# Contiguous pieces in SBUF for a fused attention and two-layer kernel: w_in, v, q/k, x and the gated tile laid out anew

## The chip, the cores and the metric

The kernel runs on one core of a Trainium2 chip. The metric is device time in microseconds. TensorE is called PE below (PEld is its weight load), VectorE DVE, ScalarE ACT, GpSimd POOL and SyncE SP. SBUF is the on-chip memory that holds the tiles, PSUM the banks into which PE writes.

## The reference

Attention over 4 batches, 8 heads, 768 positions and 64 channels a head, where each query sees the first 4 positions (the sinks) and its own last 128; then two layers with a squared ReLU between them, over all 3072 tokens.

```python
scores = (1.0 / np.sqrt(D)) * np.matmul(q, k.transpose(0, 1, 3, 2))
keep = (pos[None, :] < 4) | ((rel >= 0) & (rel < 128))       # rel = query - key
a = softmax(np.where(keep, scores, -1e9))
x = np.matmul(a, v).transpose(0, 2, 1, 3).reshape(B * S, H * D)     # 3072 x 512
h = x @ w_in                                                 # 512 x 2048
out = (np.maximum(h, 0.0) ** 2) @ w_out                      # 2048 x 512
```

## The kernel before

**Tiles.** A batch is 768 tokens: six tiles of 128 (index t), three pairs of tiles (index s), four pairs of heads (index m). For batches 0 and 1, SP loads q and k as FP32 (tile qr), they are cast and regrouped to bf16 (qs, on DVE, ACT or POOL), PE transposes them (pt), and ACT and DVE copy the result to qkT. For batches 2 and 3, the tuple NATURAL, POOL's queue loads them with a cast (qn), and SP issues DMA transposes from qn to qkT (the "turns", L416). The values come as FP32 (vf) and are cast to v, or in batches 2 and 3 straight to v by POOL's queue.

**Steps.** For each pair s and each half of the heads: scores on PE (ps, L538), exponential on ACT (expm, L557), mask by a product on DVE (L566) or by a select on POOL (L221), values on PE (po, L599), and a division by the sum on DVE (rc and xn_sb, L610 and L611). Scores of the sinks are a product of their own (pk, L498), whose left operand kblk is copied from qkT by DVE (L481), followed by the sinks' values vs (L484). The x of a pair is turned by PE (px, L634) and copied to xT, or by a DMA transpose in batches 2 and 3. The first layer is pm (L657), ReLU on ACT (r, L666), the square on DVE into gT_sb (L673). The second layer is py (L697), copied out to osb and stored by SP.

**Buffers.** The attention of a batch shares two PSUM slots (`att`) among pt, ps, po, px and pk; pm and py share two others (`den`). So the next scores wait until ACT has read the last.

**What sets the order.** The whole program is recorded as operations with costs, and `Plan.run` places them greedily by start time and key. On each engine the instructions then run strictly in that order. The attention of batch b+1 is spread between the two layers of batch b. The costs in the operations are figures of the planner; they decide the order alone. Waits are put in by the framework, for each pair of instructions whose regions of a tile it takes to overlap.

**Queues.** POOL's queue first loads w_in in four blocks of 512 columns, then w_out in four; block 0 of w_in waits for a q load, and w_out 2 waits for the q and k of batch 0's second group. The loads of batch 2 on POOL's queue stand behind the load of v for batch 1, tile 3. SP's queue carries the q, k and v of batches 0 and 1, then the stores and the turns. Semaphores DMASW0 to 7 count landings of POOL's queue in rotation (so DMASW0 to 3 are first the four blocks of w_in), DMAHW0 to 7 those of SP's.

Of the kernel before, what the change touches and what calls it, by code (L numbers as in the profile page):

```python
# [132 lines left out]
def kernel(  # L133
# [23 lines left out]
    NSINK = 4  # L157
# [18 lines left out]
    head_rows = consts.tile([32, H, 1], BF16)  # L176
    w_in_sb = consts.tile([128, NKB, DFF], BF16)
    w_out_sb = consts.tile([128, NFB, DM], BF16)
# [3 lines left out]
    vs_in = consts.tile([32, B, D + 1], FP32)  # L182
    qkT_all = [consts.tile([128, NP, 2, S], BF16, name=f"qkT{i}") for i in range(2)]
    v_sb = [consts.tile([128, H, NT, D + 1], BF16, name=f"v{i}") for i in range(2)]
    xn_sb = consts.tile([128, NT, DM], BF16)
    xT_sb = [consts.tile([128, NKB, S], BF16, name=f"xT{i}") for i in range(2)]
    gT_sb = consts.tile([128, NFB, S], BF16)

# [90 lines left out]
    def dma_op(queue, name, run, us, behind=None, takes=(), yields=()):  # L279

        def go(e):
            ds = run(e)
            if behind is not None:
                for d in ds:
                    after_dma(d, loaded[behind])
            loaded[name] = ds[-1]
        o = op(-5, {queue: (0.85 if queue == "pool" else 0.5) + (1.5 if behind else 0.0)}, go, dma=us, takes=takes,
               follow=[chained[queue]] if queue in chained else (),
               after=[ops[behind]] if behind is not None else ())
        ops[name] = chained[queue] = o  # L290
        o.yields += [ops[y] for y in yields]
        o.follow += [ops[y] for y in yields]
        return o

    def load_w_in(i, behind=None, yields=()):
        c = slice(512 * i, 512 * i + 512)
        w_in_op[i] = dma_op(
            "pool", ("w_in", i),
            lambda e: [nc.gpsimd.dma_start(out=w_in_sb[:, :, c],  # L299
                                           in_=moe_w_in[:, c].rearrange("(a p) f -> p a f", p=128))],  # L300
            3.1, behind, yields=yields)

    def load_w_out(i, behind=None, yields=()):
        w_out_op[i] = dma_op(
            "pool", ("w_out", i),
            lambda e: [nc.gpsimd.dma_start(
                out=w_out_sb[:, 4 * i:4 * i + 4, :],
                in_=moe_w_out[512 * i:512 * i + 512, :].rearrange("(p f) m -> p f m", p=128))],
            2.8, behind, yields=yields)

# [7 lines left out]
    GROUPS[0] = [(0, 4), (512, 2)]  # L318
    ROW = {256: 0.0205, 512: 0.028, 1024: 0.046, 1536: 0.065}

# [32 lines left out]
    def load_natural(b, s, older_values):  # L353

        begun = [ops["layer1", b - 2, 0, 0], w_out_op[3]]
        for ti in (1, 0):
            if s == 0:
                qn_slot[b, ti] = Slot("qr", NT)
            for i in range(2):
                t = 2 * s + i  # L360

                def run(e, t=t, ti=ti):
                    if t == 0:
                        qn_t[b, ti] = work["qr"].tile([128, NT, DM], BF16, name="qn", tag="qr")
                    return [nc.gpsimd.dma_start(  # L365
                        out=qn_t[b, ti][:, t, :].rearrange("p (h d) -> p h d", d=D),
                        in_=(q, k)[ti][b, :, 128 * t:128 * t + 128, :].rearrange("h p d -> p h d"))]
                o = dma_op("pool", ("qk", b, ti, t), run, 64 * 0.032,
                           ("v", 1, 3) if (b, ti, t) == (2, 1, 0) else None,
                           [qn_slot[b, ti]] if t == 0 else ())  # L370
                o.after += begun
        for t in (2 * s, 2 * s + 1):
            def run(e, t=t):
                return [nc.gpsimd.dma_start(  # L374
                    out=v_sb[b % 2][:, :, t, 0:D],
                    in_=v[b, :, 128 * t:128 * t + 128, :].rearrange("h p d -> p h d"))]
            o = dma_op("pool", ("v", b, t), run, 64 * 0.032)
            o.after += begun + older_values
# [6 lines left out]
    def attention(b, key):  # L385
# [9 lines left out]
        older_layer1 = [ops[x] for x in ops if x[0] == "layer1" and x[1] == b - 2]  # L395
        qkT_sb = qkT_all[b % 2]
        es, vs, vb, kb, xT = es_sb[b % 2], vs_sb[b % 2], v_sb[b % 2], kblk[b % 2], xT_sb[b % 2]

        def stage(g, f0, f1, side):
# [9 lines left out]
            if b in NATURAL:  # L409
                for s in range(NS):  # L410
                    for ti in (1, 0):
                        for i in range(2):
                            t = 2 * s + i

                            def turn(e, s=s, ti=ti, i=i, t=t):
                                nc.sync.dma_start_transpose(  # L416
                                    out=qkT_sb[:, :, ti, 128 * t:128 * t + 128], in_=qn_t[b, ti][:, t, :])
                            ops["turn", b, ti, t] = op(
                                at(0.1 * s), {"sp": 1.25}, turn, dma=0.3, reads=[qn_slot[b, ti]],
                                after=[ops["qk", b, ti, t]] + prev_scores + prev_sinks)  # L420
                            copies.append(ops["turn", b, ti, t])
                    ops["cast", b, s] = ops["v", b, 2 * s + 1]
            for m in range(NP) if b not in NATURAL else ():
# [31 lines left out]
                for ti in (1, 0):  # L455
                    def unload(e, m=m, ti=ti):

                        pt = bank_t[b, m, g]
                        copy(e,
                             qkT_sb[:, m, ti, t0:last].rearrange("c (p t) -> c p t", t=n),  # L460
                             pt[:, ti, 0:128 * n].rearrange("c (t p) -> c p t", t=n))
# [6 lines left out]
            for s in range(t0 // 256, last // 256) if b not in NATURAL else ():  # L468
                def cast(e, s=s):
                    copy(e, vb[:, :, 2 * s:2 * s + 2, 0:D].rearrange("p h t d -> p t h d"), vf_t.pop((b, s)))  # L470
                ops["cast", b, s] = op(at(0.3 + 0.5 * (256 * s - t0) / (last - t0)),
# [5 lines left out]
            if g == 0:  # L477
                def sink_operands(e):
                    for h2 in range(2):
                        r = slice(64 * h2, 64 * h2 + 64)  # L480
                        nc.vector.tensor_copy(  # L481
                            out=kb[r, :].rearrange("p (m c) -> p m c", c=136)[:, :, 4 * h2:4 * h2 + NSINK],
                            in_=qkT_sb[r, :, 1, 0:NSINK])
                    nc.vector.tensor_tensor(  # L484
# [9 lines left out]
            def sink_scores(e):  # L494
                ps = bank_t["sink", b] = bank(bk, "pk", [128, 512], FP32)
                warm(ps[:, 0:128])
                for m in range(NP):
                    nc.tensor.matmul(ps[:, 0:last - lo], lhsT=kb[:, 128 * m:128 * m + 128],  # L498
                                     rhs=qkT_sb[:, m, 0, lo:last],
                                     start=(m == 0), stop=(m == NP - 1))  # L500
# [12 lines left out]
            for s in range(t0 // 256, last // 256):  # L513
                fs = 0.36 + 0.5 * (256 * s - t0) / (last - t0)
                norms = []
                for m0 in (0, 2):
# [4 lines left out]
                    def scores(e, ms, s=s, m0=m0, banks=banks):  # L521
                        for m in ms:
# [12 lines left out]
                            for i, (o, c, qb, w) in enumerate(segs):  # L535
                                for h2 in range(2):
                                    r = slice(64 * h2, 64 * h2 + 64)
                                    nc.tensor.matmul(  # L538
                                        ps[:, h2, o:o + w],
                                        lhsT=qkT_sb[r, m, 1, 128 * c:128 * c + 128],  # L540
                                        rhs=qkT_sb[r, m, 0, 128 * qb:128 * qb + w],
                                        start=(i == 0 and not biased), stop=(i == len(segs) - 1))
# [39 lines left out]
                    def values(e, s=s, m0=m0, bo=bo):  # L582
                        po = bank_t["o", b, s, m0] = bank(bo, "po", [128, 2, 512], FP32)
                        warm(po[:, 0, 0:128])
                        for j, m in enumerate((m0, m0 + 1)):
# [3 lines left out]
                            for h2 in range(2):  # L589
                                h = 2 * m + h2  # L590
                                for i in range(2):
                                    t = 2 * s + i
                                    if t >= 1:
                                        mms.append((i, h2, x[:, h2, 256 * i:256 * i + 128], vb[:, h, t - 1, :]))
                                    mms.append((i, h2, x[:, h2, 256 * i + 128:256 * i + 256], vb[:, h, t, :]))
                                    if t >= 2:
# [22 lines left out]
                if b in NATURAL:  # L619
                    for t in (2 * s, 2 * s + 1):  # L620
                        def turn_x(e, t=t):
                            nc.sync.dma_start_transpose(out=xT[:, :, 128 * t:128 * t + 128], in_=xn_sb[:, t, :])
                        o_ = op(at(fs + 0.36), {"sp": 1.25}, turn_x, dma=0.3, after=norms + older_layer1 +
# [16 lines left out]
                def bridge_copy(e, s=s):  # L640
                    copy(e, xT[:, :, 256 * s:256 * s + 256], bank_t["x", b])
                ops["xT", b, s] = op(at(fs + 0.37), {"dve": 1.2, "act": 1.05}, bridge_copy,
# [4 lines left out]
    def layer1(b, key, fbs, c0, cw, need):  # L647
# [5 lines left out]
        def mm(e):  # L653
            pm = bank_t[tag] = bank(bs, "pm", [128, n, cw], FP32)
            for i, fb in enumerate(fbs):
                for kb in range(NKB):
                    nc.tensor.matmul(pm[:, i, :], lhsT=w_in_sb[:, kb, 512 * (fb // 4) + fb % 4:512 * (fb // 4) + 512:4],  # L657
                                     rhs=xT[:, kb, c0:c0 + cw], start=(kb == 0), stop=(kb == NKB - 1))
        a = op(key, {"pe": n * NKB * cw / 2380.0}, mm, takes=[bs],
# [11 lines left out]
        def square(e):  # L671
            r = bank_t.pop((tag, "r"))
            (nc.vector if e == "dve" else nc.gpsimd).tensor_mul(  # L673
                gT_sb[:, fbs[0]:fbs[0] + n, c0:c0 + cw], r, r)
        ops["sq", b, fbs[0], c0, cw] = op(key, {"dve": 0.7}, square, reads=[rs],
                                      after=[ra] + [ops[x] for x in ops if x[0] == "layer2" and x[1] == b - 1])

    def layer2(b, u, keys, by_part=False):
# [8 lines left out]
        for n, (i, part) in enumerate(order):  # L687
            t = 2 * u + i

            def mm(e, i=i, t=t, part=part, n=n):  # L690
# [5 lines left out]
                for fb in range(4 * part, 4 * part + 4):  # L696
                    nc.tensor.matmul(pm[:, i, :], lhsT=gT_sb[:, fb, 128 * t:128 * t + 128],  # L697
                                     rhs=w_out_sb[:, fb, :], start=(fb == 0), stop=(fb == NFB - 1))
# [127 lines left out]
```

## Time and profile before

| | |
|---|---|
| time, median of 3 runs | 242.93 us (240.55 to 243.56) |
| the profiled execution's own time | 241.31 us |
| its span | 239.6 us |
| PE busy | 224.4 us, 94% |
| ACT, DVE, POOL busy | 115.1, 106.9, 53.8 us |
| first layer pm, 576 matmuls | 89.8 us busy |
| second layer py, 384 matmuls | 89.0 us busy |

PE is the busy engine, but its share is a mean: the page's slices show it idle in two places, and there another engine or a transfer ends last. Busy time also holds matmuls that ran at half clock. The span is the time from the first to the last instruction; 1.7 us of the execution's time lie outside it.

### The profile page before, as it was taken

How to read it: one execution, taken by the hardware profiler on the slowest of the kernel's cores; microseconds unless marked ns; L12 is line 12 of the kernel's file. 1: busy time of each engine (PE TensorE's matmuls, PEld its weight loads, DVE VectorE, ACT ScalarE, POOL GpSimd, SP SyncE). 2: the span in 40 equal slices, each digit the busy share in tenths (PEclk: the TensorE clock that was granted, in tenths of full speed). 3: DMA queues.
4: the chain of work that ended last, by engine and by line, in shares of the span. 5: the costliest groups of instructions: out<-in, count | busy, mean ns of one | idle time of the engine just before them, and what ended most of it. 6: DMA issues, size and time to landing. Idle time of an engine off the chain costs nothing.

```text
span 239.6 us, 4590 instructions
## 1 busy us (share of the span) xinstructions
PE 224.4 (94%) x1944; PEld 142.8 (60%) x1944; DVE 106.9 (45%) x199; ACT 115.1 (48%) x130; POOL 53.8 (22%) x74
## 2 busy tenths in 40 slices
PE   7994699999999769999999999999999999999993
PEld 7654599545994355555458754559645644694441
DVE  5676033335687763656335633857402422431010
ACT  2583056640764764955348445686604226560020
POOL 5250050520693497175000004100000000000000
PEclk9999599999999997999999999999999999999999
DMA  5999899998599999999977513120002512000042
GB/s 186 281 207 209 181 254 175 335 307 159 179 145 108 134 166 150 126 148 151 139 81 206 105 22 80 54 44 4 0 0 73 171 22 90 0 0 3 0 176 88
DMA packets 82021, 29.70 MB, mean 124 GB/s; under 512 B 70224, under 2 KB 78416, under 8 KB 82000
## 3 DMA queue, kind: packets, MB, share of 16 engines
q0 software_dynamic: 40128, 8.92, 44.7%
q1 hardware_dynamic: 41832, 20.48, 37.9%
q8 instruction: 15, 0.25, 0.4%
q14 instruction: 6, 0.05, 0.1%
q10 hardware_dynamic: 40, 0.01, 0.0%
HBM read 27.30 MB, written 6.29 MB: 140 GB/s over the span
## 4 chain that ended last, share of the span: by engine, by line
PE 84%; DMA 8%; ACT 3%; DVE 2%; POOL 1%; issue 1%; ACTq 0%
PE pm L657 36%; PE py L697 34%; DMA w_in_sb<-in_moe_w_in_dram 5%; PE po L599 5%; PE ps L538 4%; DMA qr<-in_q_dram 3%; ACT expm L557 2%; PE pt L448 1%; PE pk L498 1%; POOL w_in_sb L299 1%; PE px L634 1%; ACT xT L205 0%; ACT r L666 0%; DVE vs L234 0%; DVE xn_sb L611 0%
## 5 line engine op out<-in xcount | busy, mean ns | idle before, releaser
L657 PE MATMUL pm<-xT,w_in_sb 128*128 128x256 bf16 (+1 forms) x576 | 89.8, 314 | 5.3 <-DMA w_in_sb<-in_moe_w_in_dram 4.9
L697 PE MATMUL py<-w_out_sb,gT_sb 128*128 128x512 bf16 x384 | 89.0, 379 | 0.0
L657 PEld LDWEIGHTS <-w_in_sb 128*128 128x128 bf16 x576 | 63.7, 116 | 26.8 <-issue 7.3
L666 ACT ACTIVATE r<-pm 128x1024 bf16<-128x1024 f32 x48 | 49.3, 1027 | 52.5 <-PE pm L657 45.3
L697 PEld LDWEIGHTS <-gT_sb 128*128 128x128 bf16 x384 | 35.6, 98 | 40.2 <-issue 2.1
L673 DVE TENSOR_TENSOR gT_sb<-r 128x1024 bf16<-128x1024 bf16 x48 | 33.8, 704 | 48.2 <-ACT r L666 48.2
L557 ACT ACTIVATE expm<-ps 128x1024 bf16<-128x1024 f32 (+1 forms) x48 | 43.4, 959 | 15.4 <-PE ps L538 15.2
L566 DVE TENSOR_TENSOR expm<-expm,mask 128x1024 bf16<-128x1024 bf16 (+1 forms) x37 | 24.0, 654 | 23.4 <-ACT expm L557 23.1
L205 ACT ACTIVATE osb<-py 128x1024 f32<-128x1024 f32 (+1 forms) x10 | 9.6, 960 | 39.9 <-PE py L697 33.5
L599 PEld LDWEIGHTS <-expm 128*128 128x128 bf16 x352 | 17.7, 98 | 5.1 <-issue 2.0
L599 PE MATMUL po<-v,expm 128*128 128x65 bf16 x352 | 18.8, 196 | 1.2 <-ACT xT L205 1.1
L538 PE MATMUL ps<-qkT 64*128 64x128 bf16 (+1 forms) x256 | 15.1, 238 | 2.7 <-ACT expm L557 1.5
L611 DVE TENSOR_TENSOR xn_sb<-po,rc 128x512 bf16<-128x512 f32 x24 | 16.6, 691 | 0.8
L538 PEld LDWEIGHTS <-qkT 64*128 64x128 bf16 x256 | 8.2, 94 | 13.6 <-issue 11.0
L209 POOL CAST qs<-qr 128x256 bf16<-128x256 f32 (+1 forms) x12 | 7.3, 634 | 38.3 <-PE pt L448 20.8
L610 DVE RECIPROCAL rc<-po 128x8 f32<-128x8 f32 x24 | 5.0, 207 | 20.8 <-PE po L599 20.8
L207 DVE COPY osb<-py 128x1024 f32<-128x1024 f32 (+2 forms) x4 | 3.6, 892 | 23.6 <-PE py L697 23.6
L599 PE MATMUL po<-vs,es 128*128 128x65 bf16 x128 | 14.1, 195 | 0.0
L599 PEld LDWEIGHTS <-es 128*128 128x128 bf16 x128 | 12.3, 101 | 0.0
L365 POOL DMA_DIRECT2D qn<-in_q_dram x12 | 10.8, 912 | 6.0 <-DMA qn<-in_k_dram 6.0
L374 POOL DMA_DIRECT2D v<-in_v_dram x12 | 11.0, 919 | 4.0 <-PE ps L538 1.4
L569 POOL TENSOR_TENSOR expm<-expm,mask 128x768 bf16<-128x768 bf16 x2 | 3.7, 1858 | 32.7 <-ACT expm L557 32.7
(50 smaller groups left out, 112.0 us busy)
## 6 DMA issues: line engine op xcount, KB each, us to landing
out_dram<-osb SPq DMA_DIRECT2D x11, 512.0 KB, 3.0
vf<-in_v_dram SPq DMA_DIRECT2D x12, 256.0 KB, 6.1
w_in_sb<-in_moe_w_in_dram POOLq DMA_DIRECT2D x4, 512.0 KB, 10.0
w_out_sb<-in_moe_w_out_dram POOLq DMA_DIRECT2D x4, 512.0 KB, 11.2
qr<-in_k_dram SPq DMA_DIRECT2D x2, 768.0 KB, 5.7
qr<-in_q_dram SPq DMA_DIRECT2D x2, 768.0 KB, 7.3
qn<-in_k_dram POOLq DMA_DIRECT2D x12, 128.0 KB, 9.6
qn<-in_q_dram POOLq DMA_DIRECT2D x12, 128.0 KB, 10.6
```

Source lines behind the costliest of these rows:

```text
L205: nc.scalar.activation(out=dst, in_=src, func=AF.Copy)
L365: return [nc.gpsimd.dma_start(out=qn_t[b, ti][:, t, :].rearrange("p (h d) -> p h d", d=D), in_=(q, k)[ti][b, :, 128 * t:128 * t + 128, :]. ...
L374: return [nc.gpsimd.dma_start(out=v_sb[b % 2][:, :, t, 0:D], in_=v[b, :, 128 * t:128 * t + 128, :].rearrange("h p d -> p h d"))]
L538: nc.tensor.matmul(ps[:, h2, o:o + w], lhsT=qkT_sb[r, m, 1, 128 * c:128 * c + 128], rhs=qkT_sb[r, m, 0, 128 * qb:128 * qb + w], start=(i = ...
L557: nc.scalar.activation(out=x[:, :, o:512], in_=bank_t["s", b, s, m][:, :, o:512], func=AF.Exp, scale=scale)
L566: nc.vector.tensor_mul(x[:, :, o:512], x[:, :, o:512], mk[:, :, o:512])
L599: nc.tensor.matmul(pv[:, i, h2, :], lhsT=lhsT, rhs=rhs, start=(n_ == 0), stop=(n_ == len(mms) - 1))
L611: nc.vector.tensor_tensor(out=xn_sb[:, 2 * s:2 * s + 2, 128 * m0:128 * m0 + 256].rearrange("p i (j h d) -> p j i h d", j=2, d=D), in0=pv[: ...
L657: nc.tensor.matmul(pm[:, i, :], lhsT=w_in_sb[:, kb, 512 * (fb // 4) + fb % 4:512 * (fb // 4) + 512:4], rhs=xT[:, kb, c0:c0 + cw], start=(k ...
L666: nc.scalar.activation(out=r, in_=bank_t.pop(tag), func=AF.Relu)
L673: (nc.vector if e == "dve" else nc.gpsimd).tensor_mul(gT_sb[:, fbs[0]:fbs[0] + n, c0:c0 + cw], r, r)
L697: nc.tensor.matmul(pm[:, i, :], lhsT=gT_sb[:, fb, 128 * t:128 * t + 128], rhs=w_out_sb[:, fb, :], start=(fb == 0), stop=(fb == NFB - 1))
```

## The change

Five SBUF layouts are changed, and with them the access patterns of everything that writes or reads the tiles. The number of instructions on PE stays the same, and so does what each computes. Three cost figures of the planner are changed as well, so the greedy order comes out differently.

```diff
-    w_in_sb = consts.tile([128, NKB, DFF], BF16)
+    w_in_sb = consts.tile([128, 4, NKB, 512], BF16)
-    qkT_all = [consts.tile([128, NP, 2, S], BF16, name=f"qkT{i}") for i in range(2)]
-    v_sb = [consts.tile([128, H, NT, D + 1], BF16, name=f"v{i}") for i in range(2)]
+    qkT_all = [consts.tile([128, NP * 2 * S], BF16, name=f"qkT{i}") for i in range(2)]
+    v_sb = [consts.tile([128, NT, H, D + 1], BF16, name=f"v{i}") for i in range(2)]
-    xT_sb = [consts.tile([128, NKB, S], BF16, name=f"xT{i}") for i in range(2)]
-    gT_sb = consts.tile([128, NFB, S], BF16)
+    xT_sb = [consts.tile([128, NS, NKB, 256], BF16, name=f"xT{i}") for i in range(2)]
+    gT_sb = [consts.tile([128, NFB, w], BF16, name=f"gT{i}") for i, w in enumerate((512, 256))]
...
-        o = op(-5, {queue: (0.85 if queue == "pool" else 0.5) + (1.5 if behind else 0.0)}, go, dma=us, takes=takes,
+        o = op(-5, {queue: (0.85 if queue == "pool" else 0.5) + (0.3 if behind else 0.0)}, go, dma=us, takes=takes,
...
-            lambda e: [nc.gpsimd.dma_start(out=w_in_sb[:, :, c],
+            lambda e: [nc.gpsimd.dma_start(out=w_in_sb[:, i],
...
-            2.8, behind, yields=yields)
+            2.6, behind, yields=yields)
...
-    ROW = {256: 0.0205, 512: 0.028, 1024: 0.046, 1536: 0.065}
+    ROW = {256: 0.0205, 512: 0.028, 1024: 0.046, 1536: 0.068}
...
-        qkT_sb = qkT_all[b % 2]
+        if b in NATURAL:
+            qkT_sb = qkT_all[b % 2].rearrange("p (t i m c) -> p m i t c", t=NT, i=2, m=NP)
+        else:
+            qkT_sb = qkT_all[b % 2].rearrange("p (m i t c) -> p m i t c", t=NT, i=2, m=NP)
...
-                                    out=qkT_sb[:, :, ti, 128 * t:128 * t + 128], in_=qn_t[b, ti][:, t, :])
+                                    out=qkT_sb[:, :, ti, t, :], in_=qn_t[b, ti][:, t, :])
...
-                    nc.tensor.matmul(pm[:, i, :], lhsT=w_in_sb[:, kb, 512 * (fb // 4) + fb % 4:512 * (fb // 4) + 512:4],
-                                     rhs=xT[:, kb, c0:c0 + cw], start=(kb == 0), stop=(kb == NKB - 1))
+                    nc.tensor.matmul(pm[:, i, :], lhsT=w_in_sb[:, fb // 4, kb, fb % 4:512:4],
+                                     rhs=xT[:, c0 // 256:(c0 + cw) // 256, kb, :], start=(kb == 0), stop=(kb == NKB - 1))
...
-                gT_sb[:, fbs[0]:fbs[0] + n, c0:c0 + cw], r, r)
+                gT_sb[c0 // 512][:, fbs[0]:fbs[0] + n, c0 % 512:c0 % 512 + cw], r, r)
```

The remaining lines index the new layouts in the same way.

On PE, at the end of batch 0's first attention and the start of its first layer, the program before reads as follows (po is the last values product, pm the first layer).

```order
L599 LDWEIGHTS es_100
L599 MATMUL po<-vs_98,es_100 128x65
L657 LDWEIGHTS w_in_sb [waits DMASW0_49]
L657 MATMUL pm<-xT_108,w_in_sb 128x256 [waits Activation_49]
L657 LDWEIGHTS w_in_sb [waits DMASW3_49,DMASW2_49,DMASW1_49]
L657 MATMUL pm<-xT_108,w_in_sb 128x256
```

After the change the second weight load has no wait; the 16 matmuls of block 0 and the eight of px follow each other, and then PE comes to block 1.

```order
L639 LDWEIGHTS xn_sb
L639 MATMUL px<-ident,xn_sb 128x128
L662 LDWEIGHTS w_in_sb [waits DMASW1_49]
L662 MATMUL pm<-xT_108,w_in_sb 128x256 [waits PE_49]
L662 LDWEIGHTS w_in_sb
```

The wait for all of blocks 1 to 3 is gone from the second weight load, and one wait for each block stands where that block is first used (block 2 after 16 more matmuls, block 3 after a further 64).

On DVE, in batch 1's attention, the piece around the copy of batch 2's kblk (kblk_96) reads so before. Its wait is for the landing of the first turn of batch 2.

```order
L481 COPY kblk_96<-qkT_103 64x4x4 [waits DMAHW0_49]
L481 COPY kblk_96<-qkT_103 64x4x4
L484 TENSOR_TENSOR vs_98<-vs_in,head_rows 32x520 [waits DMAHW4_49]
L566 TENSOR_TENSOR expm<-expm,mask_90 128x2x384 [waits Activation_49] x2
L207 COPY osb<-py 128x1024 [waits DMAHW6_49,PE_49]
L610 RECIPROCAL rc<-po 128x8 [waits PE_49]
L611 TENSOR_TENSOR xn_sb<-po,rc 128x2x2x128 [waits DVE_49]
L566 TENSOR_TENSOR expm<-expm,mask 128x1024 [waits Activation_49] x3
```

After the change it reads so.

```order
L485 COPY kblk_96<-qkT_103 64x4x4 [waits DMAHW0_49]
L485 COPY kblk_96<-qkT_103 64x4x4
L488 TENSOR_TENSOR vs_98<-vs_in,head_rows 32x520 [waits DMAHW4_49]
L570 TENSOR_TENSOR expm<-expm,mask_90 128x2x384 [waits Activation_49] x2
L570 TENSOR_TENSOR expm<-expm,mask 128x1024 [waits Activation_49] x2
L614 RECIPROCAL rc<-po 128x8 [waits PE_49]
L615 TENSOR_TENSOR xn_sb<-po,rc 128x2x2x128 [waits DVE_49]
```

The copy and its wait keep their place, ahead of the masks of batch 1's pair 0, second half of the heads; an output copy leaves DVE, and two masks of pair 1 move ahead of the division.

On POOL, among the loads of batch 2, before:

```order
L374 DMA v_105<-in_v_dram 128x8x64 [waits DMASW2_49]
L374 DMA v_105<-in_v_dram 128x8x64 [waits DMASW3_49]
L221 AFFINE_SELECT expm<-expm 128x4x128 [waits Activation_49]
L221 AFFINE_SELECT expm<-expm 128x4x128
L365 DMA qn<-in_k_dram 128x8x64 [waits DMASW4_49]
```

After:

```order
L374 DMA v_105<-in_v_dram 128x8x64 [waits DMASW2_49]
L374 DMA v_105<-in_v_dram 128x8x64 [waits DMASW3_49]
L365 DMA qn<-in_k_dram 128x8x64 [waits DMASW4_49]
L365 DMA qn<-in_k_dram 128x8x64 [waits DMASW5_49]
L365 DMA qn<-in_q_dram 128x8x64 [waits DMASW6_49]
```

The two selects that masked one tile on POOL are gone from between the loads; DVE makes that mask.

## Rows read from the trace of the kernel before

**Rows 1.** Windows: busy PE, PEld, DVE, ACT, POOL (count), clock, DMA share, GB/s.
```profile
24.18:31.00 6.82, 5.04 (x28) 3.89 (x29) 0.58 (x1) 1.64 (x2) 0.00 (x0) 0.50 0.91 198
...
81.60:91.74 10.14, 6.46 (x114) 5.26 (x114) 6.60 (x12) 6.48 (x7) 9.45 (x12) 0.87 1.67 151
...
42.87:79.98 37.11, 37.11 (x349) 23.70 (x346) 22.15 (x41) 19.57 (x26) 16.59 (x19) 1.00 1.43 201
91.74:239.60 147.86, 143.63 (x1092) 83.63 (x1090) 57.45 (x95) 67.39 (x72) 15.95 (x16) 1.00 0.57 76
```

**Rows 2.** The chain that ended last: start us, us, what.
```profile
13.15 12.68 DMA w_in_sb<-in_moe_w_in_dram
...
25.96 3.37 PE pm L657 x15
29.33 0.85 PE px L634 x8
30.18 12.69 PE pm L657 x112
42.87 0.86 PE py L697 x4
...
62.80 3.49 PE pm L657 x32
...
104.49 3.46 PE pm L657 x16
```

**Rows 3.** Timeline, start us, us, instruction, idle before it and who ended that.
```profile
20.78 0.27 PE L657 MATMUL pm<-xT,w_in_sb 128*128 128x256 bf16 x1
...
61.92 0.83 POOL L209 CAST qs<-qr 128x768 bf16<-128x768 f32 x1 [10.61 <-PE pt L448]
...
62.70 1.78 POOL L365 DMA_DIRECT2D qn<-in_k_dram  x2
...
69.69 6.07 SPq L416 DMA_TRANSPOSE qkT<-qn  x4
...
77.69 0.35 DVE L481 COPY kblk<-qkT 64x16 bf16<-64x16 bf16 x2 [1.08 <-DMA qkT<-qn]
...
78.69 1.09 DVE L566 TENSOR_TENSOR expm<-expm,mask 128x768 bf16<-128x768 bf16 x2
...
81.07 0.53 PE L599 MATMUL po<-v,expm 128*128 128x65 bf16 x12
```

**Rows 4.** Tile w_in_sb, blocks 1 and 2: duration, start, then issue to landing.
```profile
L299 POOL DMA_DIRECT2D w_in_sb<-in_moe_w_in_dram x1: 748/748/748, 11.7 to 11.7; - x1
...
DMA to landing us min/median/max: 9.1/9.1/9.1
...
L299 POOL DMA_DIRECT2D w_in_sb<-in_moe_w_in_dram x1: 750/750/750, 12.4 to 12.4; - x1
...
DMA to landing us min/median/max: 10.9/10.9/10.9
```

**Rows 5.** Tile qn, the load issued at 62.70: issue to landing.
```profile
DMA to landing us min/median/max: 6.9/6.9/6.9
```

**Rows 6.** Tile vf, batch 1's v loads of token tiles 2 and 4, likewise.
```profile
L348 SPq DMA_DIRECT2D vf<-in_v_dram x1: 3477/3477/3477, 48.8 to 48.8; - x1
...
DMA to landing us min/median/max: 7.2/7.2/7.2
...
L348 SPq DMA_DIRECT2D vf<-in_v_dram x1: 1000/1000/1000, 53.4 to 53.4; - x1
...
DMA to landing us min/median/max: 5.3/5.3/5.3
```

**Rows 7.** Issue to landing, whole run: qn's 24 loads, qkT's 24 turns, xT's 12.
```profile
DMA to landing us min/median/max: 5.3/10.6/14.2
...
DMA to landing us min/median/max: 3.3/8.2/9.5
...
DMA to landing us min/median/max: 2.4/2.5/3.6
```

More of the change, by code (lines that the diff above doesn't have):

```diff
@@ L374, in run @@
                 return [nc.gpsimd.dma_start(
-                    out=v_sb[b % 2][:, :, t, 0:D],
+                    out=v_sb[b % 2][:, t, :, 0:D],
                     in_=v[b, :, 128 * t:128 * t + 128, :].rearrange("h p d -> p h d"))]
@@ L459, in unload @@
                         copy(e,
-                             qkT_sb[:, m, ti, t0:last].rearrange("c (p t) -> c p t", t=n),
+                             qkT_sb[:, m, ti, t0 // 128:last // 128, :].rearrange("c a b -> c (a b)").rearrange(
+                                 "c (p t) -> c p t", t=n),
                              pt[:, ti, 0:128 * n].rearrange("c (t p) -> c p t", t=n))
@@ L469, in cast @@
                 def cast(e, s=s):
-                    copy(e, vb[:, :, 2 * s:2 * s + 2, 0:D].rearrange("p h t d -> p t h d"), vf_t.pop((b, s)))
+                    copy(e, vb[:, 2 * s:2 * s + 2, :, 0:D], vf_t.pop((b, s)))
                 ops["cast", b, s] = op(at(0.3 + 0.5 * (256 * s - t0) / (last - t0)),
@@ L482, in sink_operands @@
                             out=kb[r, :].rearrange("p (m c) -> p m c", c=136)[:, :, 4 * h2:4 * h2 + NSINK],
-                            in_=qkT_sb[r, :, 1, 0:NSINK])
+                            in_=qkT_sb[r, :, 1, 0, 0:NSINK])
                     nc.vector.tensor_tensor(
@@ L498, in sink_scores @@
                     nc.tensor.matmul(ps[:, 0:last - lo], lhsT=kb[:, 128 * m:128 * m + 128],
-                                     rhs=qkT_sb[:, m, 0, lo:last],
+                                     rhs=qkT_sb[:, m, 0, lo // 128:last // 128, :],
                                      start=(m == 0), stop=(m == NP - 1))
@@ L539, in scores @@
                                         ps[:, h2, o:o + w],
-                                        lhsT=qkT_sb[r, m, 1, 128 * c:128 * c + 128],
-                                        rhs=qkT_sb[r, m, 0, 128 * qb:128 * qb + w],
+                                        lhsT=qkT_sb[r, m, 1, c, :],
+                                        rhs=qkT_sb[r, m, 0, qb:qb + w // 128, :],
                                         start=(i == 0 and not biased), stop=(i == len(segs) - 1))
@@ L593, in values @@
                                     if t >= 1:
-                                        mms.append((i, h2, x[:, h2, 256 * i:256 * i + 128], vb[:, h, t - 1, :]))
-                                    mms.append((i, h2, x[:, h2, 256 * i + 128:256 * i + 256], vb[:, h, t, :]))
+                                        mms.append((i, h2, x[:, h2, 256 * i:256 * i + 128], vb[:, t - 1, h, :]))
+                                    mms.append((i, h2, x[:, h2, 256 * i + 128:256 * i + 256], vb[:, t, h, :]))
                                     if t >= 2:
@@ L621, in turn_x @@
                         def turn_x(e, t=t):
-                            nc.sync.dma_start_transpose(out=xT[:, :, 128 * t:128 * t + 128], in_=xn_sb[:, t, :])
+                            nc.sync.dma_start_transpose(out=xT[:, t // 2, :, 128 * (t % 2):128 * (t % 2) + 128],
+                                                        in_=xn_sb[:, t, :])
                         o_ = op(at(fs + 0.36), {"sp": 1.25}, turn_x, dma=0.3, after=norms + older_layer1 +
@@ L640, in bridge_copy @@
                 def bridge_copy(e, s=s):
-                    copy(e, xT[:, :, 256 * s:256 * s + 256], bank_t["x", b])
+                    copy(e, xT[:, s], bank_t["x", b])
                 ops["xT", b, s] = op(at(fs + 0.37), {"dve": 1.2, "act": 1.05}, bridge_copy,
@@ L696, in mm @@
                 for fb in range(4 * part, 4 * part + 4):
-                    nc.tensor.matmul(pm[:, i, :], lhsT=gT_sb[:, fb, 128 * t:128 * t + 128],
+                    nc.tensor.matmul(pm[:, i, :], lhsT=gT_sb[t // 4][:, fb, 128 * (t % 4):128 * (t % 4) + 128],
                                      rhs=w_out_sb[:, fb, :], start=(fb == 0), stop=(fb == NFB - 1))
```

## The prediction

> **What bounds the kernel now.** I read the windows first, to see where PE isn't busy. From 42.87 to 79.98 us it has no idle time at all, and from 91.74 to the end only 4.2 us in 147.9 [rows 1]. That leaves two places. The first is around 21 to 31 us. The timeline shows one matmul of the first layer at 20.78, and the chain shows the next fifteen at 25.96, released by the last load of w_in, which was issued at 13.15 and took 12.68 us [rows 2, 3]. So PE stood for some 4.9 us after a single matmul of block 0, waiting for block 3, which those fifteen matmuls don't read. From 24.18 to 31.00 the granted clock is 0.50, the lower of the two levels (1.2 against 2.4 GHz), after PE had been idle [rows 1]; the fifteen matmuls take 3.37 us, where 32 of the same shape take 3.49 us later [rows 2]. The second place is 81.60 to 91.74, where PE is busy 6.5 of 10.1 us [rows 1]: batch 1's attention without any layer work left to put between its steps, so that the two PSUM slots and ACT pace it. Everything else is PE in a row, so what is saved before 80 us moves the end, unless something that doesn't move with PE is then late.
>
> **Part 1, the wait for w_in.** With a block contiguous, the weight loads wait block by block, as the order shows. At full clock a matmul of this shape costs 3.49/32 = 0.109 us, and the eight of px half of their 0.85 us at half clock, 0.43 [rows 2]. Starting at 20.78 as now, block 0 ends at 22.5 and px at 23.0; then block 1 is wanted, which landed at 11.7 + 9.1 = 20.8; block 2 at 24.7, landed at 12.4 + 10.9 = 23.3; block 3 at some 31.7, landed at 13.15 + 12.68 = 25.8 [rows 2, 4]. No wait is left. The 128 matmuls and px end at 20.78 + 128 x 0.109 + 0.43 = 35.2 us, where they end at 42.87 now [rows 2]: **7.7 us earlier**. Of this about 5 us are the wait, and some 2.5 us are the half clock (5.04 us busy at half rate [rows 1]). The blocks of w_out don't move with PE either; no idle time of PE ends with them now [rows 1], and I put nothing on them, but count them among what could be late.
>
> **Part 2, the order up to 82 us.** The planner's new costs shuffle PE between there and the end of the values product at 81.07 + 0.53 = 81.6 [rows 3], but the count of each shape of matmul up to that place (96 second layer, 64 first layer, 64 pt, and so on) is the same in both orders. PE did them without idle time [rows 1], so unhindered the same set ends at 81.6 - 7.7 = 73.9. What doesn't move with PE is the load chain. In DVE's queue the copy of batch 2's kblk waits for the first turn of batch 2, and behind it in the queue stand the masks of batch 1's pair 0, which the values product (po) needs. Now this wait costs DVE 1.08 us and PE nothing [rows 3]. After the change PE and DVE come there 7.7 us sooner. The chain is: POOL issues the first k load of batch 2 at 62.70, after a cast that had waited for PE; it lands 6.9 us later; SP's turn goes at 69.69 and has landed by 77.69 [rows 3, 5], 15.0 us in all. POOL will reach that issue sooner too, since its casts follow PE's transposes, but no sooner than the v load of tile 3 lands, behind which it is put: between tile 2's 48.8 + 7.2 = 56.0 and tile 4's 53.4 + 5.3 = 58.7 [rows 6], say 57.3. SP's queue up to there depends on loads, not on PE, so I leave it. The turn then lands at 57.3 + 15.0 = 72.3. Both masks are done 2.1 us after the landing now (79.78 against 77.69 [rows 3]), so at 74.4, and the second half of the product needs 0.27 more: 74.7. In the new order four matmuls of the second layer (0.86 us [rows 2]) come after this product, so it would end unhindered at 73.0. **PE waits 1.6 us**. With the v load's two bounds the wait is 0.3 or 3.0.
>
> **Part 3, the rest.** The stretch without fillers, 81.6 to 91.74, keeps its steps; scores of pair 2 now come ahead of the first layer, and the steps are grouped by two. Its length is set by exponentials and slots, so I leave it as it is, with 1 us less to 2 us more as ends. POOL's two selects leave its queue, and batch 2's and 3's later loads come earlier by more than PE does; nothing on PE waited for them. After 91.74 the same work is left, and the 4.2 us of idle there [rows 1], which lies mostly in the end of the program, stays. The new patterns cost nothing that I can find: weights keep their stride, and a 512-column matmul whose moving operand is in two pieces of 256 can cost no more than two of 256, 0.218 against 3.46/16 = 0.216 [rows 2], which for the 192 such matmuls is 0.4 us at most. DVE and ACT write contiguous runs of the same length of work; from 42.87 to 79.98 DVE is busy 22.15 of 37.11 us [rows 1], so a gain there has no one to wait for it.
>
> **The sum.** 7.7 - 1.6 = 6.1 us off. The profiled execution took 241.31 us, which gives 235.2; it lies 1.6 us under the median, and the mean of the four times shown is 242.1, so I forecast **236.0 us**, and 234.7 to 237.4 by the v load's bounds.
>
> **Rivals.** *The turns land sooner.* Turns of x have the same shape, four pieces of 128 tokens, and land in 2.5 us when the queues are quiet, against 8.2 for those of q and k among the loads [rows 7]. If a good part of the 8 us is the turn's own strided writing, a contiguous destination takes it away; from a landing time of 6.3 us down PE's wait is gone, and the time is 242.1 - 7.7 = 234.4, or 233.4 with the shorter attention. Against it: x's turns wrote strided pieces too and were fast, so it is the loads around the turn that make it slow, and I keep 8 us. The Trainium skill, "DMA: Bandwidth & Descriptors", section "Latency and other measured facts", speaks for this rival: it gives 261 GB/s for a DMA transpose with a non-contiguous middle dimension and about 350 to 400 where it is contiguous. By that ratio the turn would be an estimated 5.6 us and the sum would come out here; no run here has shown it.
>
> *The wait grows to what was saved.* After the change batch 2's first load comes while v loads and two stores are on SP's queue. If it takes the median of its kind, 10.6, and the turn 8.2 [rows 7], the landing is at 76.1 and the wait 5.4 us. A wait as long as the one of 4.9 us now was followed by half clock for 5.04 busy us, which lost 2.5 [rows 1]. Then the time is 242.1 - 7.7 + 5.4 + 2.5 = 242.3, or 239.8 if the clock holds: no change that one can measure.
>
> *Slower.* It is the same place and the same DVE wait, with the longest of each, 14.2 and 9.5 [rows 7]: landing at 81.0, wait 10.3, half clock 2.5, 247.2 us. The loss passes the gain when the landing is after 75.9. For it speaks that SP's and POOL's queues are both full at that time; against it, that a first load of a burst took 6.9 [rows 5] and only late ones took longest.
>
> *The change doesn't do what it says* can be left out: the waits are seen to be gone from the order.
>
> **Chances.** Forecast 0.50, turns sooner 0.20, wait grown 0.22, slower 0.06, other 0.02. The range takes the second case whole and half of the third: 233.0 to 240.8. About 2% (4.9 us, so 238.1) is what a measurement of this kernel tells from no change. Forecast and first rival lie under it, nearly whole: faster 0.68; the third case and the forecast's tail give the same 0.26; slower 0.06.
>
> **What would show it.** Step 1: first-layer matmuls in a row from about 20.8 us with the second layer at about 35.2, no wait on w_in, no half clock at 24 to 31. Step 2: DVE's kblk copy idle for some 5 us until about 72.3 for a turn, then PE's values product about 1.6 us late. Step 3: a stretch of some 10 us with PE two thirds busy, ending near 86. I'm wrong if w_in's blocks land later than now, if batch 2's first load is issued well after 58.7, or if PE meets a new wait between 35 and 73, where the steps of batch 0's second group now stand closer together.

## The result and the profile after

The changed kernel takes **234.12 us** (median of four runs, 233.5 to 235.98), where the kernel before takes 242.66 beside it: ratio 0.967 (95% interval 0.959 to 0.976), so faster. Measured again later, beside the last experiments, it is 235.14 us and 0.972 (0.967 to 0.977). Here and below a median counts every run, while a ratio compares only runs in the faster of two states that both kernels fall into, so the two can differ by half a per cent. The profiled execution after took 234.2 us with a span of 232.5, so 7.1 us less than the one before.

The page after, busy times, and the line of the granted clock in 40 slices:

```profile
PE 219.4 (94%) x1924; PEld 140.5 (60%) x1944; DVE 107.3 (46%) x201; ACT 116.7 (50%) x131; POOL 49.3 (21%) x70
...
PEclk9999999999999999999999999999999999999999
```

The clock is full in every slice, where the mean was 0.978 before. PE's busy time is 5.0 us less, but most of that is no gain: 17 of py's 384 records are missing from this trace, some 4 us at 0.235 each (86.3 us for 367). Windows after, columns as in [rows 1]:

```profile
20.99:35.58 14.59, 14.59 (x140) 14.56 (x139) 7.29 (x19) 8.09 (x8) 2.71 (x6) 1.00 1.02 219
24.18:31.00 6.82, 6.82 (x65) 6.82 (x63) 2.58 (x4) 4.40 (x5) 0.00 (x0) 1.00 0.94 204
...
72.30:85.50 13.20, 8.60 (x145) 5.79 (x144) 9.24 (x19) 7.85 (x9) 7.00 (x8) 1.00 2.02 161
85.50:232.50 147.00, 141.75 (x1069) 83.23 (x1080) 55.98 (x94) 67.75 (x73) 13.13 (x15) 1.00 0.60 79
```

From 24.18 to 31.00 PE did 5.04 us of work at clock 0.50 before [rows 1]; now it is busy throughout at 1.00. The chain of waits, start us, us, what:

```profile
19.92 1.03 ACT xT L205
20.95 0.04 issue
20.99 1.91 PE pm L662 x16
22.90 0.45 PE px L639 x8
23.35 12.23 PE pm L662 x112
35.58 0.45 PE pt L451 x8
...
63.07 9.21 DMA qkT<-qn
72.28 0.02 issue
72.30 0.17 DVE kblk L485
...
72.68 0.69 DVE vs L488
73.37 2.14 DVE expm L570 x4
...
85.11 0.40 PE ps L542 x6
85.50 3.58 PE pm L662 x16
```

No load of w_in is in it any more: the first layer begins when x is turned and copied, and its 128 matmuls and px run as one row until 35.58, where they ended at 42.87 [rows 2]. Then the chain shows the longer wait at DVE's copy of kblk. The timeline there, start us, us, what, idle before and who ended it:

```profile
58.09 1.78 POOL L365 DMA_DIRECT2D qn<-in_k_dram  x2 [3.71 <-DMA vf<-in_v_dram]
...
63.07 12.29 SPq L419 DMA_TRANSPOSE qkT<-qn  x5
...
71.37 1.67 PE L702 MATMUL py<-w_out_sb,gT 128*128 128x512 bf16 x7 [0.16 <-issue]
72.30 0.35 DVE L485 COPY kblk<-qkT 64x16 bf16<-64x16 bf16 x2 [4.66 <-DMA qkT<-qn]
...
73.89 0.82 PE L603 MATMUL po<-v,expm 128*128 128x65 bf16 x12 [0.85 <-DVE expm L570]
```

DVE stood 4.66 us for the first turn of batch 2, where it stood 1.08 before [rows 3]. PE had been done with its work at 73.04 (71.37 + 1.67) and then waited 0.85 us for the masks that are queued behind the copy. PE's waits by cause over the whole run, us in total, times, longest:

```profile
PE po L603 <- DVE expm L570: 1.1, 2, 0.8
PE ps L542 <- ACT expm L561: 1.0, 2, 0.5
```

The first row is two waits; the other one, 0.2 us, is at 82.5 and has nothing to do with the copy.

Issue to landing of qkT's 24 turns, min, median and max:

```profile
DMA to landing us min/median/max: 2.4/8.0/8.9
```

They were 3.3, 8.2 and 9.5 [rows 7].

**Where the 7.1 us come from, by places.** First layer of batch 0 done: 42.87 to 35.58, 7.3 us. First layer of batch 1 begun: 91.74, and 0.55 more for twelve scores that now come ahead of it, to 85.50, 6.8 us. End: 239.6 to 232.5. So all of it is made in front, some 0.5 us is lost up to 85.5, and 0.3 regained behind.

### The profile page after: what moved, and what is told of

Read it like the earlier page. It is cut to its first block, busy times and chain, and to the rows that moved or that the text cites. A ratio compares the mean times of both kernels' runs of the same rounds, so it can differ in the third digit from the quotient of the medians.

```text
span 232.5 us, 4566 instructions
## 1 busy us (share of the span) xinstructions
PE 219.4 (94%) x1924; PEld 140.5 (60%) x1944; DVE 107.3 (46%) x201; ACT 116.7 (50%) x131; POOL 49.3 (21%) x70
## 4 chain that ended last, share of the span: by engine, by line
PE 79%; ACT 7%; DMA 7%; DVE 4%; issue 1%; SPq 1%; ACTq 0%
PE pm L662 36%; PE py L702 31%; ACT expm L561 4%; PE po L603 4%; DMA qkT<-qn 4%; PE ps L542 3%; DMA qr<-in_k_dram 3%; DVE expm L570 2%; PE pt L451 2%; ACT xT L205 1%; PE px L639 1%; PE pk L502 1%; SPq L331 1%; ACT qkT L205 1%; DVE xn_sb L615 1%
## 5 line engine op out<-in xcount | busy, mean ns | idle before, releaser
L702 PE MATMUL py<-w_out_sb,gT 128*128 128x512 bf16 x367 | 86.3, 379 | 1.3 <-issue 0.6
L662 PE MATMUL pm<-xT,w_in_sb 128*128 128x256 bf16 (+1 forms) x576 | 86.9, 308 | 0.4 <-ACT r L671 0.2
L662 PEld LDWEIGHTS <-w_in_sb 128*128 128x128 bf16 x576 | 62.9, 114 | 20.7 <-issue 2.0
L702 PEld LDWEIGHTS <-gT 128*128 128x128 bf16 x384 | 35.7, 98 | 39.6 <-issue 1.6
L678 DVE TENSOR_TENSOR gT<-r 128x1024 bf16<-128x1024 bf16 x48 | 33.1, 691 | 40.5 <-ACT r L671 40.5
L570 DVE TENSOR_TENSOR expm<-expm,mask 128x1024 bf16<-128x1024 bf16 (+1 forms) x40 | 26.8, 677 | 27.4 <-ACT expm L561 26.8
L205 ACT ACTIVATE osb<-py 128x1024 f32<-128x1024 f32 (+1 forms) x12 | 11.6, 970 | 34.4 <-PE py L702 28.0
L603 PEld LDWEIGHTS <-expm 128*128 128x128 bf16 x352 | 16.7, 97 | 6.2 <-DVE expm L570 2.1
L365 POOL DMA_DIRECT2D qn<-in_k_dram x12 | 10.6, 886 | 7.9 <-DMA vf<-in_v_dram 3.7
L205 ACT ACTIVATE qkT<-pt 128x512 bf16<-128x512 bf16 (+2 forms) x11 | 6.5, 625 | 11.4 <-PE pt L451 10.0
```

Source lines behind the costliest of these rows:

```text
L205: nc.scalar.activation(out=dst, in_=src, func=AF.Copy)
L365: return [nc.gpsimd.dma_start(out=qn_t[b, ti][:, t, :].rearrange("p (h d) -> p h d", d=D), in_=(q, k)[ti][b, :, 128 * t:128 * t + 128, :]. ...
L570: nc.vector.tensor_mul(x[:, :, o:512], x[:, :, o:512], mk[:, :, o:512])
L603: nc.tensor.matmul(pv[:, i, h2, :], lhsT=lhsT, rhs=rhs, start=(n_ == 0), stop=(n_ == len(mms) - 1))
L662: nc.tensor.matmul(pm[:, i, :], lhsT=w_in_sb[:, fb // 4, kb, fb % 4:512:4], rhs=xT[:, c0 // 256:(c0 + cw) // 256, kb, :], start=(kb == 0), ...
L678: (nc.vector if e == "dve" else nc.gpsimd).tensor_mul(gT_sb[c0 // 512][:, fbs[0]:fbs[0] + n, c0 % 512:c0 % 512 + cw], r, r)
```

## The experiments

Theory A is the prediction's: w_in's layout makes the gain, by the wait for all blocks and the half clock behind it. Rival B: the planner's new order gains by itself. Rival C: the other four layouts gain, by turns that land sooner or by copies.

**w_in alone.** The kernel before with three lines changed:

```diff
-    w_in_sb = consts.tile([128, NKB, DFF], BF16)
+    w_in_sb = consts.tile([128, 4, NKB, 512], BF16)
...
-            lambda e: [nc.gpsimd.dma_start(out=w_in_sb[:, :, c],
+            lambda e: [nc.gpsimd.dma_start(out=w_in_sb[:, i],
...
-  lhsT=w_in_sb[:, kb, 512 * (fb // 4) + fb % 4:512 * (fb // 4) + 512:4]
+  lhsT=w_in_sb[:, fb // 4, kb, fb % 4:512:4]
```

> The kernel before with w_in alone in the new layout; the other four layouts and the planner's figures, so also the order on every engine, are those of before. Theory A (the gain is the wait for w_in's later blocks and the half clock behind it): the second layer starts near 35.5 us instead of 42.87, the granted clock stays at 1.00 between 24 and 31, and the time is 234 to 236.5 us, ratio 0.965 to 0.975. Rival B (a good part of the gain is in the new order or in the other layouts): the front moves the same 7 us, but 3 us or more are given back before 92 us, and the time is 238 or more, ratio 0.98 or more.

Measured 235.25 us, ratio 0.972 (0.964 to 0.979): 6.9 us, nearly the whole gain. Its chain in front:

```profile
20.46 1.91 PE pm L657 x16
22.37 0.45 PE px L634 x8
22.82 12.23 PE pm L657 x112
35.05 0.22 PE py L697
```

The wait is gone and the row is as in the changed kernel. The marks are theory A's: the second layer starts at 35.05, and the time is in its range. The stretch without layer work to fill PE's gaps ran mostly at the lower clock in this execution, which the changed kernel's first profile does not show:

```profile
76.90:87.10 10.20, 8.27 (x96) 6.20 (x94) 5.26 (x10) 4.81 (x5) 5.75 (x7) 0.50 2.07 168
```

**All but w_in.** The changed kernel with the three lines above put back.

> The changed kernel with w_in alone put back into the old layout. Theory A: the wait of about 5 us and the half clock come back, nothing else was worth more than 1 us: 241 to 243 us, ratio 0.993 to 1.003. Rival B: the new order and the four other layouts keep 2 us or more of the gain: 240.5 us or less, ratio under 0.99.

Measured 240.42 us, ratio 0.990 (0.986 to 0.995; ten runs). Both lie at the edge that was set for rival B (240.5 us, 0.99) and below theory A's range: what the rest of the change gives without w_in's layout is small, but not nothing. The next run has the order without any layout.

**The three cost figures alone,** on the kernel before:

```diff
-  + (1.5 if behind else 0.0)
+  + (0.3 if behind else 0.0)
...
-            2.8, behind, yields=yields)
+            2.6, behind, yields=yields)
...
-    ROW = {256: 0.0205, 512: 0.028, 1024: 0.046, 1536: 0.065}
+    ROW = {256: 0.0205, 512: 0.028, 1024: 0.046, 1536: 0.068}
```

> The kernel before with the three figures of the planner alone, so the new order on all engines with the old layouts. Theory A: 241 to 243 us, ratio 0.993 to 1.003, like the kernel before. Rival B: 240.5 us or less, ratio under 0.99. A third way, that the old layouts' extra waits bite in the new order: 244 us or more.

Measured 240.75 us, ratio 0.989 (0.981 to 0.998), the same as with the four layouts; by the ratio this is rival B's range and not theory A's. So without w_in's layout the rest of the change is worth some 2.5 us, and the order alone accounts for it. Its longest wait on PE, and two windows (columns as above):

```profile
PE pm L657 <- DMA w_in_sb<-in_moe_w_in_dram: 3.9, 1, 3.9
```

```profile
26.60:30.00 3.40, 3.40 (x22) 2.61 (x21) 0.18 (x1) 1.23 (x2) 0.00 (x0) 0.50 0.91 189
...
80.00:90.72 10.72, 6.98 (x128) 5.17 (x128) 6.33 (x13) 7.42 (x8) 6.11 (x7) 1.00 2.15 162
```

In this order PE comes to the first layer about a microsecond later, for a load that lands at the same 25.8, so it stands 3.9 us and not 4.9, and was at half clock for 3.4 us and not 6.8. The first layer ends at 42.07, 0.8 sooner than before. The profiled span is 2.0 us shorter (237.6); the other 1.2 us come behind, where the stretch up to batch 1's first layer has a clock of 1.00 in this profile and 0.87 before [rows 1].

**PE kept busy during the wait,** which takes away the half clock and leaves the wait. The kernel before, with 88 extra matmuls whose result is overwritten:

```diff
+            if tag == (0, 0, 0):
+                for _ in range(88):
+                    nc.tensor.matmul(pm[:, 0, 0:128], lhsT=ident, rhs=ident, start=True, stop=True)
             for i, fb in enumerate(fbs):
```

> The kernel before, with 88 extra 128-column matmuls of the identity into the first layer's first bank ahead of its first matmul, about 0.056 us each, so that PE is busy while it would wait for w_in; nothing is left out and the wait stays. If the half clock of 24 to 31 us is a cost of its own (theory A, 2.5 of the 7.7 us), the first layer's matmuls after 25.9 run at full clock, the second layer starts near 40.4 and the time is 239 to 240.5 us, ratio near 0.99. If the clock falls all the same or costs nothing (rival), it starts near 42.9 and the time is that of before, ratio 1.00.

Measured 240.38 us, ratio 0.988 (0.982 to 0.995): 2.9 us. The chain:

```profile
22.69 5.07 PE pm L657 x88
27.76 1.75 PE pm L660 x16
29.51 0.45 PE px L634 x8
29.95 12.23 PE pm L660 x112
```

The first 16 matmuls take 1.75 us where 15 took 3.37, and px 0.45 for 0.85 [rows 2]. In this run the loads of w_in came a microsecond later and the extra matmuls ended 0.9 us after the last of them, so the front ends at 42.18, only 0.7 us ahead of the kernel before and not at the 40.4 that was expected; without these 1.9 us it would be 40.3. This profile has no half clock later on either, which the kernel before has at 81.60 to 91.74 [rows 1], so the 2.9 us need not all be the front's.

**The same with the new order.** The extra matmuls and the three cost figures together.

> The kernel before with 88 extra matmuls on PE while it waits for w_in (their result is overwritten) and the three new cost figures. If the new order gains by fewer stretches at half clock alone: with PE at full clock in front already, the time of the extra matmuls alone, 240.4 us, ratio 0.985 to 0.99, at a granted clock of 1.0. If the order gains by itself, whatever the clock: 2.3 to 2.6 us less than with the extra matmuls alone, 237.8 to 238.3, ratio about 0.98.

Measured 239.35 us, ratio 0.989 (0.985 to 0.993), against 0.988 without the new figures, so the first of the two expectations holds by the ratio: once PE is kept at full clock in front, no gain of the order is seen. The two profiled executions, the run without the figures first:

```profile
core 0: 238.4 us, clock 1.000
```

```profile
core 0: 236.9 us, clock 1.000
...
21.77 5.07 PE pm L657 x88
```

Both are at full clock throughout and 1.5 us apart, but 0.9 of that is a head start: the extra matmuls begin at 21.77 and not at 22.69, since a load of v landed sooner (17.63 and not 18.54). That the order's 2.5 us are less time at half clock fits these runs; that the other 0.6 us are its own is not excluded.

**The layouts without the new order.** The changed kernel with the old cost figures.

> The changed kernel with the three figures of the planner put back: all five new layouts in the order of before. Against w_in alone it differs by the four other layouts only. Theory A: the same as w_in alone within 1 us, 234 to 236.5 us, ratio 0.965 to 0.975. Rival B1 (the other layouts take away waits that matter): 1.5 us or more under w_in alone. Rival B2 (the order gives a part): 1.5 us or more above the changed kernel, 235.7 or more.

Measured 236.69 us, ratio 0.981 (0.974 to 0.987), against 0.972 (0.964 to 0.979) for w_in alone in the same order. This misses theory A's range and meets the mark of B2: with all five layouts in place the new order would be worth 2 to 3 us (0.981 against 0.967 and 0.972), though the intervals overlap. The other four layouts give no gain in this pair; whether they cost something is not resolved.

**w_in and the new order, without the other four layouts,** and the changed kernel again beside it.

> The kernel before with w_in by column block and the three new cost figures; v, q/k, x and gated tile keep their old layouts. If the other four layouts do nothing: the time of the changed kernel, 234.1 us, ratio to before 0.965 to 0.970, and the same markers in the trace (second layer from about 35.6, batch 1's first layer from about 85.5). If contiguous pieces pay (copies on DVE and ACT, turns): slower than the changed kernel by 0.5 us or more, 234.8 to 236, and turns of q and k that land later than 8.0 us in the median. If they cost (the first run with all layouts and old costs was 1.4 us above w_in alone): 232.5 to 233.5.

> The changed kernel itself, beside the two others on the same chip: 234.1 us, ratio 0.96 to 0.975. It is the value that w_in with the new costs is compared with.

Measured 236.1 us, ratio 0.976 (0.972 to 0.981), and 235.14 us, ratio 0.972 (0.967 to 0.977). In the profile the marks are those of the changed kernel (second layer at 35.5, batch 1's first layer at 85.8). To the letter the time meets what was expected if contiguous pieces pay, slower by 0.5 us or more. But the difference of 1 us has the other sign than that of the pair before, and the intervals overlap: no gain and no cost of the other four layouts is shown. Against w_in alone (0.972) the order gives nothing here, where the run before had it at 2 to 3 us with all layouts; what it adds to w_in's layout stays open. The turn that the chain goes over, with strided pieces and then, in the changed kernel, with contiguous ones:

```profile
63.92 8.46 DMA qkT<-qn
```

```profile
63.59 9.04 DMA qkT<-qn
```

The medians of all 24 are 8.3 and 8.6; over all eleven profiles of this case they are 7.8 to 8.7 with strided pieces and 7.6 to 8.6 with contiguous ones. A turn into contiguous pieces lands no sooner here. In the changed kernel's second profile the DVE wait is longer than in the first:

```profile
PE po L603 <- DVE expm L570: 1.8, 1, 1.8
```

**The copy of kblk put behind the masks,** in the changed kernel, by one dependence more for the planner. DVE's order changes there; that of PE, ACT, POOL and SP does not.

```diff
-  older_values + [c_sinks, ops["vs_in", b]])
+  older_values + [c_sinks, ops["vs_in", b]] + ([ops["values", 1, 1, 0]] if b == 2 else []))
```

> The changed kernel with one thing moved: on DVE the copy of batch 2's kblk, with its wait for the first turn, and the product behind it stand after the masks of batch 1's pair 0 and the two divisions behind them, instead of ahead of the masks; the order on PE, ACT, POOL and SP is the same. Theory A (that wait holds up PE's values products by about 1.3 us in the changed kernel): PE's wait on the masks near 73 us is gone, the first layer of batch 1 starts 1 to 1.5 us sooner than at 85.5, and the time is some 1.2 us lower, ratio to the kernel before 0.960 to 0.967. Rival (the stretch behind it is paced by exponentials and slots and takes the gain up): the wait is gone, but the first layer starts within 0.4 us of 85.5 and the time is that of the changed kernel.

Measured 234.69 us, ratio 0.971 (0.965 to 0.978). That is not told apart from the changed kernel (0.967 and 0.972), but neither from the 0.967 that theory A allowed: 1.2 us is half a per cent, and the interval is 0.7 wide to either side. PE's timeline:

```profile
84.19 3.64 PE L662 MATMUL pm<-xT,w_in_sb 128*128 128x512 bf16 x16
...
101.83 1.02 PE L502 MATMUL pk<-qkT,kblk 128*128 128x512 bf16 x4 [1.90 <-issue]
```

Without the wait batch 1's first layer begins at 84.19, where the timelines of the changed kernel's two profiles have it at 85.44 and 85.81: 1.25 and 1.6 us sooner, as theory A had it and against the rival. But then the sinks' product pk of batch 2 stands 1.90 us and starts at 101.83, later than in the changed kernel:

```profile
101.02 1.03 PE L502 MATMUL pk<-qkT,kblk 128*128 128x512 bf16 x4
```

The chain there goes over a turn and a piece without a cause:

```profile
92.42 8.08 DMA qkT<-qn
100.50 1.33 issue
```

The semaphores in the same trace give the cause. PE also waits there for the last turn of batch 2's q, which was issued at 93.73 and landed at 101.74. In the changed kernel's two profiles that turn landed at 98.13 and 99.51, 2.9 and 1.9 us ahead of pk. The lateness began before the moved copy: already the first turn of batch 2 goes at 64.89 in this execution and not at 63.07 or 63.59, so 1.8 and 1.3 us later, and the last one 3.0 and 1.3 us later (93.73 for 90.77 and 92.43):

```profile
64.89 11.11 SPq L419 DMA_TRANSPOSE qkT<-qn  x5
```

So the run shows that the wait at the first turn costs the start of batch 1's first layer 1.25 to 1.6 us. What this is worth at the end it does not settle: the times do not resolve it, and the one profile has a load chain that was late from its start.

## Why the prediction was right

The time forecast was 236.0 us and is 234.1 to 235.1; faster was right, and so was the mechanism of Parts 1 and 2. The profiled execution was put at 235.2 us and took 234.2: Part 1 gave 0.4 less than forecast, Part 2 cost some 0.75 less, and the rest gave some 0.65.

- **Part 1, the wait for w_in.** Forecast: second layer at 35.2, 7.7 us sooner. Measured: the 128 matmuls end at 35.58, 7.3 sooner. The 0.4 is a start at 20.99 and not 20.78, and 1.91 us for the first 16 where I had 1.74. That w_in alone does it is shown by the first run. The split, about 5 us wait and 2.5 half clock, agrees with the run that kept PE busy (2.9 us, interval 1.2 to 4.5), with the reservation made there.
- **Part 2, the wait on the turn.** Forecast: issue of the first k load at 57.3, landing of the turn at 72.3, PE unhindered at 73.0, 1.6 us of wait. Measured: 58.09, 72.28, 73.04, and a wait of 0.85 in one profile and 1.8 in another. The landing was hit partly by luck: the issue was 0.8 late, the load faster (landed by 63.07, 5.0 us, not 6.9) and the turn slower (9.2 us). Masks and product then followed the landing sooner than put: the product began 1.6 us behind it and not 2.1. That the wait is also the price at the end, as the sum has it, is not shown: with the wait taken away batch 1's first layer begins 1.25 to 1.6 us sooner, but the run that did this could not show it in the time.
- **Part 3, the rest at nothing.** This is the term that was mis-sized. The profiled gain is 7.1 us, Part 1 less Part 2 is 7.3 - 0.85 = 6.45, so the rest gave some 0.65. By its own run the order alone is worth some 2.5 us, and I had put it at nothing. In its profile it gains where PE was at half clock before, in front and in the stretch behind; the layout of w_in takes the front part away already. The two don't seem to add: 0.972 and 0.989 would give 0.961, and w_in with the order measured 0.976, the changed kernel 0.967 and 0.972; only the first interval of the changed kernel reaches down to 0.961. How the 0.65 splits between the order and the clock of the stretch up to 85.5 (1.00 in this profile, 0.87 before [rows 1]) stays open. That stretch itself came out as step 3 had it: PE busy 8.60 of 13.20 us, its end at 85.50.
- **The rivals.** *Turns land sooner* is refuted: 7.6 to 8.6 us in the median with contiguous pieces, 7.8 to 8.7 with strided ones. The rule of the Trainium skill that spoke for it ("DMA: Bandwidth & Descriptors", section "Latency and other measured facts") doesn't show in these transfers. *The wait grows* and *slower* needed a landing at 76 or later; it was at 72.28 and, in the second profile, 72.63. Of the rivals of the experiments, C has two pairs of runs of opposite sign and no gain to show. B is shown for a kernel that still has the wait for w_in (0.989); on top of w_in's layout one pair shows no gain (0.972 without the order, 0.976 with it) and one pair 2 to 3 us (0.981 without, 0.967 and 0.972 with), so its share there is open.

## What to carry to other kernels

When a load in pieces ends in one wait for all of them, look at the tile's layout before the transfers: pieces that interleave in SBUF were taken to overlap with each reader, and laying each piece out as one region gave 6.9 of the 7 to 8 us here, while the last block landed as before (25.70 us, 25.83 before). Price such a wait with the half clock that follows it, and do not simply add the gain of a second change that shortens the same stretch. Before removing the next wait, look at the later transfers of the same chain: here the last turn had 2.9 and 1.9 us to spare in two profiles and came 1.8 us too late in a third.

## What the runs showed of the hardware that was not expected

The spread from run to run goes with the granted clock, but not strictly. Of the kernel before, 31 runs were taken beside the experiments: 239.6 and 240.5 us in the two with a mean clock of 0.991 and 0.992, 241.0 to 242.0 in the eleven at 0.977 to 0.979, and 241.5 to 244.4 in the seven at 0.964 and 0.965. The fastest of all, though, 239.57, had 0.982, and at 0.971 one took 241.1 and another 243.4. One microsecond less of idle time on PE (3.9 against 4.9) was followed by half as long at the lower level (3.4 against 6.8 us); yet 2.2 us of idle time, in the run with all but w_in, was followed by 3.4 us as well. And the same program meets the lower level at other places in other runs: the changed kernel's stretch up to 85.5 us has a clock of 1.00 in its first profile and 0.87 in its second.

```profile
PE pm L662 <- DMA w_in_sb<-in_moe_w_in_dram: 2.2, 1, 2.2
```

```profile
72.30:85.50 13.20, 8.36 (x137) 6.38 (x138) 9.35 (x19) 6.84 (x9) 7.35 (x9) 0.87 2.02 152
```
